# The first quarter of the values loaded on ScalarE's DMA queue, ahead of the bias rows

## The chip, the cores and the metric

The kernel runs on one core of a Trainium2 chip. The metric is device time in microseconds of one execution, as the median of several runs: 118.21 us for the kernel before (three runs, 117.67 to 118.22).

## The reference

Softmax attention in its linear form, for 8 batches, 8 heads, 576 positions and head size 64, followed by a gated ("highway") layer on the 4608 x 512 result:

```python
def _attn_ref(q, k, v):
    q_s = softmax(q, axis=-1)
    k_s = softmax(k, axis=2)            # over the positions
    kv = np.einsum('bhsd,bhse->bhde', k_s, v)
    return np.einsum('bhsd,bhde->bhse', q_s, kv)

def _moe_ref(x, w_h, w_t, b_t):
    H = np.maximum(x @ w_h, 0.0)
    T = 1.0 / (1.0 + np.exp(-(x @ w_t + b_t)))
    return T * H + (1.0 - T) * x
```

`q`, `k`, `v` and the output are float32; the kernel computes in float16 with float32 sums.

## The kernel before, in words

The whole program is one list of steps, `ORDER`. A step is named `kind_batch_part`, with an engine's letter behind a colon where the engine can be chosen (`A` ScalarE, `D` VectorE, `P` GpSimd). The steps are issued in that order, each engine's instructions keep it, and every engine waits for what the instruction at its head needs. The words below use these step names.

Per batch, the steps are: `k`, `v`, `q` load rows from memory (lines 269, 292); `ek` and `eq` take the exponentials on ScalarE (lines 339, 397); `vc` casts the values to float16 (line 345); `kv` multiplies keys by values on TensorE (line 355); `kr` and `kn` normalise that product on VectorE (lines 367, 377); `qt` and `qc` turn the queries, on TensorE and then by a copy (lines 441, 452); `xu`, `rs`, `x` make the attention output (lines 496, 511, 523); `xt` and `xe` turn it (lines 542, 553). The layer behind it is `bw` (gate bias into PSUM, line 564 on TensorE), `mt` and `mh` (the two products, lines 574 and 582), `th`, `dd`, `uu`, `oo`, and `st` (the stores).

In batch 0 the loads come in pieces: two of the queries, `q_0_0` (512 KB) and `q_0_4` (640 KB); two of the keys, `k_0_0` and `k_0_2` (576 KB each); and four of the values, `v_0_0` to `v_0_3` (288 KB each). All go out on SyncE (SP in the profile). The bias row of 2 KB is loaded twice, `b_0` and `b_32` (line 300, into two partitions), on ScalarE's queue. ScalarE and SyncE each have a DMA queue of their own: q10 and q1 in the profile.

What the bias does next: VectorE casts both rows and subtracts (`bsplit`, lines 323 and 324); TensorE spreads the result over the partitions (`bp`, line 330); ScalarE copies it to `ball` (`bc`, line 333). On TensorE `bp` stands behind 13 dummy products (`fill_5`, `fill_8`, line 253) and ahead of `qt_0_0`, two `bw`, eight more dummy products and `kv_0_0`. On VectorE `bsplit` stands ahead of the cast of `v_0_1` and of `qc_0_0`.

Every DMA of SyncE and ScalarE takes one of eight semaphores in turn, so a DMA waits at its issue for the one eight before it to land.

Of the kernel before, what the change touches and what calls it, by code (L numbers as in the profile page):

```python
# [13 lines left out]


ORDER = """
b_0 q_0_0 v_0_1 setupdve k_0_0 b_32 eq_0_0 bsplit setuppool fill_5 fill_8 bp v_0_0 bc qt_0_0 ek_0_1 v_0_3 ek_0_0 k_0_2
v_0_2 vc_0_3:A bw_1 vc_0_0 ek_0_2 vc_0_2 q_0_4 vc_0_1:D ek_0_3 bw_0 w_h_0 fill_8 qc_0_0 whd_1:P kv_0_0 eq_0_1 w_h_2
w_t_2 kr_0_0 whd_0:P whd_2:P wtb_2:P bw_2:D fill_4 w_t_0 q_1_4 k_1_2 kn_0_0 v_1_2 xu_0_0 kv_0_1 kr_0_1 fill_5 kn_0_1
xu_1_0 rs_1_0 k_1_0 wtb_0:P qt_0_1 qc_0_1:A x_1_0 xt_1_0 xe_1_0 xu_0_1 wtb_1:P fill_2 whb_2 v_1_0 whb_1:D rs_0_0 whb_0  # L20
# [45 lines left out]
def kernel(  # L66
# [10 lines left out]
    nc = tc.nc  # L77
# [35 lines left out]
    def once(name, make):  # L113
        if name not in T:
            T[name] = make()
        return T[name]
# [143 lines left out]
    def landing(which, b):  # L260
        return once(f"{which}32{b}", lambda: ld.tile([P, 4, NJ * D], FP32, tag=which, name=f"{which}32_{b}"))

    def rows_of(which, b):
        return source[which][b].rearrange("(c hh) (p j) d -> (hh p) c (j d)", hh=2, p=NP)

    def load_kv(which):
        def step(e, b, c):
            n = (2 if which == "k" else 1, 2)[b] if b < 2 else 4
            nc.sync.dma_start(landing(which, b)[:, c:c + n], rows_of(which, b)[:, c:c + n])
        return step  # L270

    WIDE = (4, 5, 6, 7)
# [363 lines left out]
    def st(e, i, h):  # L636
# [21 lines left out]
        setuppool=setup_pool, setuplate=setup_late, setupdve=setup_dve, bsplit=bsplit, fill=fill,  # L658
# [38 lines left out]
```

## Time and profile before

| What | us |
|---|---|
| median of the runs before | 118.21 |
| runs before, lowest and highest | 117.67, 118.22 |
| the profiled execution, its own time | 118.84 |
| its span in the trace | 117.0 |

The profile page gives each engine's busy time, the share that the DMA engines were busy, and the chain of work that ended last. A row of the timeline is: start in us, duration in us, engine, line, operation, out<-in, and in brackets how long the engine sat idle before it and what ended the wait. "SPq" and "ACTq" rows are DMA issues. In the windows view a row names a stretch and its length, then the busy time of each engine, the granted TensorE clock, the mean busy share of the 16 DMA engines and what they moved in GB/s. The DMA view of a window lists the queues with packets, megabytes and share.

### The profile page before, as it was taken

How to read it: one execution, taken by the hardware profiler on the slowest of the kernel's cores; microseconds unless marked ns; L12 is line 12 of the kernel's file. 1: busy time of each engine (PE TensorE's matmuls, PEld its weight loads, DVE VectorE, ACT ScalarE, POOL GpSimd, SP SyncE). 2: the span in 40 equal slices, each digit the busy share in tenths (PEclk: the TensorE clock that was granted, in tenths of full speed). 3: DMA queues.
4: the chain of work that ended last, by engine and by line, in shares of the span. 5: the costliest groups of instructions: out<-in, count | busy, mean ns of one | idle time of the engine just before them, and what ended most of it. 6: DMA issues, size and time to landing. Idle time of an engine off the chain costs nothing.

```text
span 117.0 us, 3825 instructions
## 1 busy us (share of the span) xinstructions
PE 105.7 (90%) x1544; PEld 56.7 (48%) x1544; DVE 94.7 (81%) x225; ACT 90.2 (77%) x129; POOL 87.1 (74%) x101
## 2 busy tenths in 40 slices
PE   5997866998899999999999999999999989999930
PEld 1353532554556646645474547455454534454520
DVE  5544585597999899999889887997999979899870
ACT  4276393977789899998999986989999958867320
POOL 5011154068999999999899999999899918996760
PEclk9999999999999999999999999999999999999995
DMA  2999999999999999999999999999999999999654
GB/s 48 372 399 378 407 393 382 391 372 387 391 391 391 389 394 362 379 391 365 375 390 380 350 365 404 358 361 335 391 354 259 107 362 325 403 398 352 247 209 177
DMA packets 24197, 40.62 MB, mean 347 GB/s; under 512 B 5362, under 2 KB 11762, under 8 KB 24180
## 3 DMA queue, kind: packets, MB, share of 16 engines
q1 hardware_dynamic: 24032, 40.24, 98.4%
q8 instruction: 12, 0.20, 0.7%
q10 hardware_dynamic: 148, 0.14, 0.3%
q14 instruction: 5, 0.04, 0.1%
HBM read 30.41 MB, written 9.44 MB: 341 GB/s over the span
## 4 chain that ended last, share of the span: by engine, by line
PE 41%; DMA 27%; ACT 19%; DVE 6%; issue 3%; SPq 1%; DVEq 0%; ACTq 0%
DMA q<-in_q_dram 21%; PE one L582 15%; PE one L574 14%; DMA eq<-qe 6%; ACT qe L392 4%; PE one L542 3%; PE one L441 3%; ACT ek L339 3%; ACT one L598 3%; ACT eq L452 2%; PE pair L487 2%; PE pair L355 2%; ACT th L596 2%; ACT eq L454 1%; ACT xT L553 1%
## 5 line engine op out<-in xcount | busy, mean ns | idle before, releaser
L634 POOL TENSOR_TENSOR o<-u,x 128x512 f32<-128x512 f16 (+1 forms) x36 | 40.6, 1143 | 5.9 <-DVE u L616 4.5
L582 PE MATMUL one<-w16h,xT 128*128 128x512 f16 x144 | 36.4, 380 | 0.8 <-ACT xT L553 0.7
L574 PE MATMUL one<-w16t,xT 128*128 128x512 f16 (+1 forms) x148 | 36.9, 374 | 0.2 <-issue 0.2
L602 DVE SCALAR_TENSOR_TENSOR d<-x,one 128x512 f16<-128x512 f16 x36 | 24.1, 673 | 2.0 <-PE one L582 2.0
L614 POOL TENSOR_TENSOR u<-g,d 128x512 f16<-128x512 f16 x18 | 20.8, 1158 | 1.5
L345 POOL CAST v<-v 128x1152 f16<-128x1152 f32 (+1 forms) x11 | 10.6, 972 | 13.5 <-DMA v<-in_v_dram 13.1
L339 ACT ACTIVATE ek<-k 128x576 f16<-128x576 f32 (+2 forms) x15 | 17.9, 1224 | 2.4 <-DMA k<-in_k_dram 2.4
L582 PEld LDWEIGHTS <-xT 128*128 128x128 f16 x144 | 12.7, 98 | 13.7 <-ACT xT L553 1.2
L518 DVE TENSOR_TENSOR x<-pair,rs 128x512 f16<-128x512 f32 x27 | 18.2, 684 | 1.1
L574 PEld LDWEIGHTS <-xT 128*128 128x128 f16 x148 | 13.0, 98 | 11.9 <-issue 0.5
L397 ACT ACTIVATE qe<-q 128x1024 f16<-128x1024 f32 (+3 forms) x9 | 9.4, 1055 | 5.7 <-DMA q<-in_q_dram 5.7
L598 ACT ACTIVATE one<-one 128x512 f32<-128x512 f32 (+1 forms) x19 | 10.7, 562 | 3.1 <-PE one L574 2.7
L616 DVE SCALAR_TENSOR_TENSOR u<-one,d 128x512 f16<-128x512 f32 (+1 forms) x18 | 12.0, 671 | 1.2 <-ACT one L598 0.9
L253 PE MATMUL one<-blank 128*128 128x512 f16 x32 | 9.7, 454 | 2.2 <-POOL blank L143 1.3
L560 ACT COPY one<-ball 128x512 f32<-128x512 f32 x18 | 10.6, 588 | 1.4 <-DVE d L602 0.8
L596 ACT ACTIVATE th<-one 128x512 f16<-128x512 f32 x18 | 10.5, 594 | 1.1 <-PE one L574 0.9
L613 POOL TENSOR_SCALAR g<-th 128x512 f16<-128x512 f16 x18 | 11.2, 622 | 0.1
L542 PE MATMUL one<-idh,x 128*128 128x128 f16 x92 | 9.5, 220 | 1.0 <-DVE x L523 1.0
L562 DVE COPY one<-ball 128x512 f32<-128x512 f32 x13 | 8.9, 684 | 0.6 <-ACT th L596 0.5
L542 PEld LDWEIGHTS <-x 128*128 128x128 f16 x92 | 6.4, 98 | 5.9 <-DVE x L523 2.8
L392 ACT ACTIVATE qe<-q 128x1024 f16<-128x1024 f32 (+1 forms) x7 | 8.2, 1182 | 0.8 <-DMA q<-in_q_dram 0.8
L553 ACT COPY xT<-one 128x512 f16<-128x512 f16 (+1 forms) x10 | 5.5, 546 | 3.3 <-PE one L542 2.7
(68 smaller groups left out, 133.1 us busy)
## 6 DMA issues: line engine op xcount, KB each, us to landing
v<-in_v_dram SPq DMA_DIRECT2D x6, 1152.0 KB, 13.5
k<-in_k_dram SPq DMA_DIRECT2D x6, 1152.0 KB, 11.9
out_dram<-o SPq DMA_DIRECT2D x23, 256.0 KB, 3.7
q<-in_q_dram SPq DMA_DIRECT2D x10, 512.0 KB, 12.4
out_dram<-o SPq DMA_DIRECT2D x6, 512.0 KB, 4.5
k<-in_k_dram SPq DMA_DIRECT2D x4, 576.0 KB, 9.2
q<-in_q_dram SPq DMA_DIRECT2D x2, 1152.0 KB, 15.1
q<-in_q_dram SPq DMA_DIRECT2D x2, 640.0 KB, 9.7
```

The source lines that it names most:

```text
L339: nc.scalar.activation(t[:, :, c:c + n].rearrange("p j c d -> p c j d"), T[f"k32{b}"][:, c:c + n].rearrange("p c (j d) -> p c j d", j=NJ), ...
L392: nc.scalar.activation(t[:, half].rearrange("p t c d -> p c t d"), src, AF.Exp)
L518: nc.vector.tensor_mul(t.rearrange("p k (w h) e -> p w k h e", w=2), pairs(i)[:, :, :, 1:129].rearrange("p w k (h e) -> p w k h e", h=2), ...
L542: nc.tensor.matmul(t[:, n], T[f"x{i}"][:, n0 + n % 2:n0 + 2 * P:2], idh, is_transpose=True, start=True, stop=True, skip_group_check=True)
L574: nc.tensor.matmul(T[gate(i, k)][:, cs], T[f"xT{i}"][:, n], w16["t"][:, n, cs], start=False, stop=(n == parts[-1] and not first), skip_gro ...
L582: nc.tensor.matmul(t, T[f"xT{i}"][:, n], w16["h"][:, n], start=(first and n == parts[0]), stop=(n == parts[-1] and not (first and len(part ...
L596: nc.scalar.activation(T[f"th{i}"], src, AF.Tanh, scale=0.5)
L598: nc.scalar.activation(src, src, AF.Tanh, scale=0.5)
L602: nc.vector.scalar_tensor_tensor(t, T[f"x{i}"], -0.5, T[f"gps{i}"], op0=ALU.mult, op1=ALU.max)
L614: nc.gpsimd.tensor_mul(t, g, T[f"d{i}"])
L616: nc.vector.scalar_tensor_tensor(t[:, cs], T[gate(i, h)][:, cs], 1.0, T[f"d{i}"][:, cs], op0=ALU.add, op1=ALU.mult)
L634: eng.tensor_add(t[:, cs], T[f"u{i}_{h}"][:, cs], T[f"x{i}"][:, cs])
```

## The change

`v_0_1` gets the letter `A` and moves to the front of the list, and the loader takes ScalarE's queue for a step with that letter. SyncE issues one load fewer at the start, and ScalarE issues `v_0_1` ahead of the two bias rows.

```diff
 ORDER = """
-b_0 q_0_0 v_0_1 setupdve k_0_0 b_32 eq_0_0 bsplit setuppool fill_5 fill_8 bp v_0_0 bc qt_0_0 ek_0_1 v_0_3 ek_0_0 k_0_2
+v_0_1:A b_0 q_0_0 setupdve k_0_0 b_32 eq_0_0 bsplit setuppool fill_5 fill_8 bp v_0_0 bc qt_0_0 ek_0_1 v_0_3 ek_0_0 k_0_2
...
     def load_kv(which):
         def step(e, b, c):
             n = (2 if which == "k" else 1, 2)[b] if b < 2 else 4
-            nc.sync.dma_start(landing(which, b)[:, c:c + n], rows_of(which, b)[:, c:c + n])
+            (nc.scalar if e == "A" else nc.sync).dma_start(landing(which, b)[:, c:c + n], rows_of(which, b)[:, c:c + n])
         return step
```

The first rows of ScalarE's program before (a name's first number is the batch; the last is only a buffer's number):

```order
L300 DMA b_86<-in_moe_b_t_dram 1x512 x2
L397 ACT_TABLE_LOAD
L397 ACTIVATE qe_120<-q_0_101 128x4x4x64
L333 COPY ball<-one_160 128x512
L339 ACTIVATE ek_174<-k_0_117 128x9x64 x2
```

and with the change:

```order
L269 DMA v_0_100<-in_v_dram 128x576
L300 DMA b_86<-in_moe_b_t_dram 1x512 x2
L397 ACT_TABLE_LOAD
L397 ACTIVATE qe_120<-q_0_103 128x4x4x64
L333 COPY ball<-one_160 128x512
L339 ACTIVATE ek_174<-k_0_117 128x9x64 x2
```

The load of the values, 128 rows of 576 numbers, now stands ahead of the two bias loads, and nothing else moves on ScalarE.

The first rows of SyncE's program before:

```order
L292 DMA q_0_101<-in_q_dram 128x4x256
L269 DMA v_0_103<-in_v_dram 128x576
L269 DMA k_0_117<-in_k_dram 128x2x576
L269 DMA v_0_103<-in_v_dram 128x576 x2
L269 DMA k_0_117<-in_k_dram 128x2x576
L269 DMA v_0_103<-in_v_dram 128x576
L292 DMA q_0_101<-in_q_dram 128x4x320
```

and with the change:

```order
L292 DMA q_0_103<-in_q_dram 128x4x256
L269 DMA k_0_117<-in_k_dram 128x2x576
L269 DMA v_0_100<-in_v_dram 128x576 x2
L269 DMA k_0_117<-in_k_dram 128x2x576
L269 DMA v_0_100<-in_v_dram 128x576
L292 DMA q_0_103<-in_q_dram 128x4x320
```

The second row is gone; each later load is one place nearer to the front of SyncE's queue. TensorE's instructions are the same, and on VectorE and GpSimd only the number of the values' buffer differs. In the turn of eight semaphores the load of `v_0_2` (the last `v` row of SyncE above) waited for `b_0`, and now waits for `v_0_1`.

## The prediction

> **What bounds the kernel now.** I read the page first, then busy time by stage, then the chain.
>
> ```profile
> PE 105.7 (90%) x1544; PEld 56.7 (48%) x1544; DVE 94.7 (81%) x225; ACT 90.2 (77%) x129; POOL 87.1 (74%) x101
> DMA  2999999999999999999999999999999999999654
> q1 hardware_dynamic: 24032, 40.24, 98.4%
> PE 41%; DMA 27%; ACT 19%; DVE 6%; issue 3%; SPq 1%; DVEq 0%; ACTq 0%
> ```
>
> The reader should see that two resources are nearly full over the whole span: TensorE (90%) and the DMA engines (98.4% by queue q1, 9 tenths in every slice but the first and the last three). The windows (PE busy is the first column after the length, the DMA share the last but one) show where TensorE is not full:
>
> ```profile
> 0.00:14.00 14.00, 11.55 (x120) 5.36 (x120) 6.61 (x25) 7.14 (x9) 2.94 (x11) 1.00 0.88 317
> 14.00:20.00 6.00, 3.79 (x32) 2.00 (x33) 4.65 (x13) 4.01 (x8) 3.24 (x6) 1.00 1.04 390
> 20.00:30.00 10.00, 9.48 (x134) 5.44 (x132) 7.46 (x19) 7.67 (x13) 5.03 (x6) 1.00 1.06 383
> 90.00:100.00 10.00, 9.52 (x158) 4.65 (x157) 9.11 (x19) 7.58 (x12) 7.17 (x8) 1.00 0.99 261
> ```
>
> From 20 us on TensorE has at most half a microsecond idle in ten. So an event in the first 15 us, where the change lies, moves the end by about what it moves the start of that dense stretch. The chain there:
>
> ```profile
> 0.73 4.39 DMA q<-in_q_dram
> 5.14 7.81 DMA q<-in_q_dram
> 12.97 1.07 ACT qe L397
> 19.75 1.04 PE one L582 x4
> ```
>
> The reader should see that the chain runs through the landing of the second piece of the queries, not through the values that are moved: the cast of `v_0_1` (VectorE, 5.91, below) is not in it.
>
> **The change, part by part.** These rows are the start of the two queues and the bias work:
>
> ```profile
> 0.73 0.78 ACTq L300 DMA_DIRECT2D b<-in_moe_b_t_dram  x2
> 0.73 0.46 SPq L292 DMA_DIRECT2D q<-in_q_dram  x1
> 1.25 0.49 SPq L269 DMA_DIRECT2D v<-in_v_dram  x1
> 1.54 1.28 ACT L397 ACT_TABLE_LOAD   x1 [1.54 <-PEq L681]
> 4.67 0.42 DVE L323 CAST b<-b 1x512 f16<-1x512 f32 x1 [1.32 <-DMA b<-in_moe_b_t_dram]
> 5.13 0.68 DVE L324 TENSOR_TENSOR b<-b,b 1x512 f16<-1x512 f32 x1
> 4.06 0.47 SPq L269 DMA_DIRECT2D v<-in_v_dram  x1
> 5.15 1.06 ACT L397 ACTIVATE qe<-q 128x1024 f16<-128x1024 f32 x1 [2.32 <-DMA q<-in_q_dram]
> 5.91 0.75 DVE L345 CAST v<-v 128x576 f16<-128x576 f32 x1
> ```
>
> *Issue.* SyncE loses one issue of 0.49 us. That is worth nothing: SyncE's queue is issued far ahead of its data (`q_0_4`, issued at 5.14, lands 7.81 us later), so the data in front of it hide the earlier issue. For the same reason the new wait of `v_0_2` for `v_0_1` costs nothing. `v_0_1` has landed by 5.91 already now, so the issue of `v_0_2` and of what is queued behind it on SyncE (`q_0_4`, then the weights) slips at most from 4.06 to about 5.9, while GpSimd gets the data of `v_0_2` only at 11.21 (the row stands below with the other casts). ScalarE gains that 0.49 us ahead of its bias issues and its table load, which then ends near 3.3; its first work waits for the queries until 5.15 anyway. `v_0_1` landing earlier helps nobody: `kv_0_0`, the first user, starts at 9.23.
>
> *The order of the data.* This is what costs. In the DMA view for 1.9 to 4.0 us, and then for 4.0 to 4.2 us, the queues read:
>
> ```profile
> DMA packets 452, 0.47 MB, mean 222 GB/s; under 512 B 4, under 2 KB 446, under 8 KB 452
> q1 hardware_dynamic: 452, 0.47, 86.2%
> ```
>
> ```profile
> q1 hardware_dynamic: 60, 0.08, 104.3%
> q10 hardware_dynamic: 2, 0.00, 2.8%
> ```
>
> `b_32` was issued by 1.51, yet from 1.9 to 4.0 us no packet of q10 ran at all; its two packets (the row and its signal) ran after 4.0, as the first piece of the queries was ending. So a transfer of one queue waited until its DMA engine was through with the other queue's whole transfer. The last stores say the same. Here are their issues, and the queues from 114.7 to 115.2 us:
>
> ```profile
> 113.55 0.51 SPq L642 DMA_DIRECT2D out_dram<-o  x1
> 113.61 0.38 ACTq L642 DMA_DIRECT2D out_dram<-o  x1
> ```
>
> ```profile
> q10 hardware_dynamic: 119, 0.12, 68.3%
> q1 hardware_dynamic: 43, 0.04, 24.6%
> ```
>
> ScalarE's store, issued 0.06 us later, ran ahead of SyncE's in a block. I read both as: an engine takes a whole transfer of the one queue, then one of the other. With the change the turns are then `v_0_1` and `q_0_0`, `b_0`, `k_0_0`, `b_32`: the second bias row comes behind 288 KB of values and 576 KB of keys more than now. What 288 KB take is the distance of the first two landings here:
>
> ```profile
> 8.19 0.66 POOL L345 CAST v<-v 128x576 f16<-128x576 f32 x1 [5.91 <-DMA v<-in_v_dram]
> 8.91 0.67 ACT L345 CAST v<-v 128x576 f16<-128x576 f32 x1 [0.25 <-DMA v<-in_v_dram]
> 11.21 0.67 POOL L345 CAST v<-v 128x576 f16<-128x576 f32 x1 [2.35 <-DMA v<-in_v_dram]
> ```
>
> 0.72 us; three times that is 2.16. Against it stands the slow start. From 1.9 to 4.0 the engines moved 222 GB/s where 394 is the mean of 4.2 to 20 us,
>
> ```profile
> DMA packets 2967, 6.23 MB, mean 394 GB/s; under 512 B 199, under 2 KB 1251, under 8 KB 2966
> ```
>
> so 2.1 x (1 - 222/394) = 0.92 us of transfer were lost, some of which a second queue with work may fill. I take 0.3 of it, nearer to nothing than to all, since nothing shows that the gaps are the queue's and not the engines'. **The bias lands 2.16 - 0.3 = 1.86 us later**; the ends are 2.16 - 0.92 = 1.24 and, where the queries go ahead of the values on that engine and one more 288 KB comes in between, 2.88.
>
> The Trainium skill, "DMA: Bandwidth & Descriptors", section "Issuing engines are not separate DMA queues", says that issuing from several engines saves only the sequencer's issue time. By that the 0.3 would be 0 and the bias 2.16 us late; no row here shows two full queues at the start.
>
> *What a late bias delays.* On TensorE:
>
> ```profile
> 6.11 0.59 PE L330 MATMUL one<-b,ones 128*128 128x512 f16 x2
> 9.23 0.48 PE L355 MATMUL pair<-v,ek 64*64 64x65 f16 x36
> 11.09 0.28 PE L496 MATMUL one<-kvb,eq 128*128 128x130 f16 x2 [0.40 <-DVE kvb L377]
> 11.93 0.48 PE L355 MATMUL pair<-v,ek 64*64 64x65 f16 x36 [0.56 <-POOL v L345]
> 14.09 0.62 PE L441 MATMUL one<-idh,qe 128*128 128x128 f16 x8 [0.26 <-ACT qe L397]
> ```
>
> The bias is ready at 5.13 + 0.68 = 5.81, and `bp` starts at 6.11 when the dummy products end: 0.30 of cover. Behind `bp` stand `qt_0_0`, two `bw` and eight dummy products in fixed order, so `kv_0_0` moves with it, and so do VectorE's `kr` and `kn` and the `xu` of 11.09. The next product, `kv_0_1`, had waited 0.56 for its values, and `qt_0_1` 0.26 for its exponentials; both idle times are eaten first. What is left reaches the chain at 14.09: 1.86 - 0.30 - 0.56 - 0.26 = **0.74 us**; with the two ends 0.12 and 1.76. ScalarE's `bc` and `ek` slide within this. `q_0_0`, which may land up to 0.72 later behind the values, is hidden too: `qt_0_0` then stands behind the late `bp`. From there to 19.75, where the chain's row begins the dense stretch, TensorE waits often (3.79 us busy of 6), but by the view of waits on VectorE, ScalarE and its own issue and never on a load. So I take nothing off and count 0.7 to the end.
>
> **The sum.** The profiled execution took 118.84 (span 117.0 and 1.84 around it), which is 0.63 above the median. 118.84 + 0.7 = 119.5 for an execution like it, and 118.21 + 0.7 = **118.9** for the median.
>
> **The rivals.**
>
> *The queues alternate in small portions, and the start is filled* (faster). The Trainium skill's same page, section "Queues, rings and completion order", says that an engine switches queues at packets, typically 9 to 17 descriptors. As a mechanism of this kernel: ScalarE's queue holds only the 8 rows per engine of `v_0_1` ahead of the bias, so the bias would land no later than 4.67, nothing would be eaten, and the stream of loads could start up to 0.92 earlier, which moves `q_0_4` at 12.95 and the chain behind it. Half of that gives 118.21 - 0.4 = 117.8, the ends 117.3 and 118.2. For it: the share and rate at the start, 222 against 394 GB/s. Against it: the 2.1 us without a packet of q10.
>
> *The late bias is absorbed* (no change). Later idle times that a DMA ends,
>
> ```profile
> 79.10 1.06 ACT L392 ACTIVATE qe<-q 128x1024 f16<-128x1024 f32 x1 [0.55 <-DMA q<-in_q_dram]
> 94.75 0.30 PE L487 MATMUL pair<-kvl,eq 64*128 64x65 f16 x8 [0.48 <-DMA eq<-qe]
> ```
>
> could swallow 0.5 us of 0.7, if the stream of loads is not late itself: 118.4, between 118.0 and 118.8. Against it: ScalarE issues the second of those transposes only after its own work, which would be late too.
>
> **How the numbers follow.** A change of 0.5%, 0.6 us, is about what a measurement of this kernel can tell from none. The forecast has a chance of 0.55; its ends, 118.3 to 120.0, put 0.37 above 118.8 and 0.18 within 0.5%. The first rival has 0.27: 0.18 faster by over 0.5%, 0.09 within. The second has 0.18: 0.13 within, 0.05 slower. Together: faster 0.18, same 0.40, slower 0.42. The range reaches from most of the first rival's cases to the greater part of the forecast's: 117.6 to 119.7.
>
> **What would show it.** In the new profile VectorE's cast of the second bias row should start near 6.5 (from 6.0 to 7.5) instead of 4.67, `bp` near 7.7, `kv_0_0` near 10.8, the `qt` of 14.09 near 14.8, the product of 19.75 near 20.4. If the cast starts before 5 us, the turns of whole transfers are wrong. If it is late and the product of 19.75 is not, the idle times were larger than I read. If both are late and the end is not, the dense stretch has more room than its busy shares say.

## The result, and the profile after

The change makes the kernel slightly slower. The median of 22 runs is 118.42 us (118.15 to 118.66) against 118.20 us (117.67 to 119.50, 22 runs) for the kernel before. The ratio is 1.0023, with a 95% interval of 1.0012 to 1.0034: 0.27 us more, with 0.14 to 0.40 as the interval. The profiled execution took 118.21 us, with a span of 116.4. That is 0.63 less than the execution that was profiled before, so the two must not be subtracted: four executions of each kernel are laid side by side below.

From the page of the kernel with the change, the busy times, the DMA row in 40 slices, the queues, and the shares of the chain:

```profile
PE 106.0 (91%) x1544; PEld 56.6 (49%) x1544; DVE 94.4 (81%) x225; ACT 90.1 (77%) x129; POOL 86.9 (75%) x101
...
DMA  3999999999999999999999999999999999997654
...
q1 hardware_dynamic: 23888, 39.95, 97.2%
q10 hardware_dynamic: 292, 0.43, 1.1%
q8 instruction: 12, 0.20, 0.7%
...
PE 80%; DVE 8%; DMA 4%; ACT 3%; issue 1%; ACTq 1%; DVEq 0%
```

The same two resources are full. New is the chain: the share of DMA fell from 27% to 4% and TensorE's doubled. The chain of waits with the change, by start and duration, tells why:

```profile
1.76 4.47 DMA b<-in_moe_b_t_dram
...
6.25 0.43 DVE b L323
...
6.71 0.69 DVE b L324
...
7.44 0.59 PE one L330 x2
...
8.91 1.73 PE one L253 x8
10.64 0.45 PE pair L355 x33
...
20.22 1.04 PE one L582 x4
```

The path no longer starts with the queries. It starts with the bias row of 2 KB, whose landing takes 4.47 us, goes through VectorE's cast and subtraction into `bp`, and from there along TensorE through the eight dummy products to `kv_0_0`. So the moved values are still not on the path, but the bias behind them now is.

The timeline with the change at the places named in the prediction:

```profile
0.74 0.43 ACTq L269 DMA_DIRECT2D v<-in_v_dram  x1
0.74 0.47 SPq L292 DMA_DIRECT2D q<-in_q_dram  x1
1.20 0.82 ACTq L300 DMA_DIRECT2D b<-in_moe_b_t_dram  x2
...
2.05 1.28 ACT L397 ACT_TABLE_LOAD   x1 [2.05 <-issue]
...
5.05 1.06 ACT L397 ACTIVATE qe<-q 128x1024 f16<-128x1024 f32 x1 [1.72 <-DMA q<-in_q_dram]
6.25 0.42 DVE L323 CAST b<-b 1x512 f16<-1x512 f32 x1 [1.29 <-DMA b<-in_moe_b_t_dram]
...
7.44 0.59 PE L330 MATMUL one<-b,ones 128*128 128x512 f16 x2 [0.66 <-DVE b L324]
10.57 0.48 PE L355 MATMUL pair<-v,ek 64*64 64x65 f16 x36
12.42 0.28 PE L496 MATMUL one<-kvb,eq 128*128 128x130 f16 x2 [0.40 <-DVE kvb L377]
12.63 0.48 PE L355 MATMUL pair<-v,ek 64*64 64x65 f16 x36
...
14.13 0.40 PE L496 MATMUL pair<-kvb,eq 128*128 128x130 f16 x4
14.36 0.61 PE L441 MATMUL one<-idh,qe 128*128 128x128 f16 x8
```

The cast of the second bias row starts at 6.25 instead of 4.67, `bp` at 7.44 instead of 6.11, and `kv_0_0` at 10.57 instead of 9.23. `kv_0_1` has lost its wait for values and starts 0.70 later, and the `qt` of 14.09 has lost its wait for exponentials and starts 0.27 later. The queries, which the prediction let slip by up to 0.72, are not late here: their exponentials start at 5.05, against 5.15.

Where the second bias row stood can be read in the DMA view of the changed kernel for 1.9 to 4.0 us (packets, MB, share),

```profile
DMA packets 490, 0.64 MB, mean 304 GB/s; under 512 B 16, under 2 KB 370, under 8 KB 490
...
q1 hardware_dynamic: 354, 0.36, 52.6%
q10 hardware_dynamic: 136, 0.28, 41.7%
```

for 3.9 to 4.2 us,

```profile
q1 hardware_dynamic: 111, 0.11, 106.4%
q10 hardware_dynamic: 2, 0.00, 1.9%
```

for 4.2 to 5.2 us,

```profile
q1 hardware_dynamic: 235, 0.39, 109.2%
```

for 5.2 to 5.4 us,

```profile
q1 hardware_dynamic: 30, 0.07, 92.1%
q10 hardware_dynamic: 1, 0.00, 16.6%
```

and for the whole of 4.7 to 5.65 us:

```profile
DMA packets 147, 0.34 MB, mean 356 GB/s; under 512 B 0, under 2 KB 0, under 8 KB 147
```

First the values (q10) and the queries (q1) share the start, at 304 GB/s where one queue alone moved 222. Two packets of q10 follow near 4 us, the first row and its signal. From 4.2 to 5.2 us there is no packet of q10 at all, though both bias rows had been issued by 2.02: q1 moves the keys. The next packet of q10, the second row, comes after 5.2 us. So the order in which the transfers begin is the one that the prediction read: values and queries, first row, keys, second row.

But the second row does not stand behind the whole of the keys. In the trace a transfer like that of the keys ends with 16 packets of 4 bytes, one for each DMA engine, its signals. From 4.7 to 5.65 us no packet under 512 B was moved, so no engine had finished its share of the keys when the row's packet started, at 5.29. In the three other traces of the change (in the table below) it started at 5.43, 5.96 and 5.74, and the first signal of the keys followed at 5.75, 5.98 and 6.01.

The following table is read from the timelines of four executions of each kernel (start in us; the first column of each four is the profiled execution of that kernel; the others are e1, e14 and e15 of before, and e9, e12 and e13 of the change, all told below):

```
                        before                       with the change
1st bias row, cast       3.00  3.00  3.00  3.00       4.55  4.72  5.09  5.01
2nd bias row, cast       4.67  4.75  4.99  4.87       6.25  6.10  6.58  6.41
queries, exponentials    5.15  5.25  5.63  4.67       5.05  5.16  5.49  5.74
bp                       6.11  5.93  6.18  6.08       7.44  7.29  7.77  7.59
kv_0_0                   9.23  9.07  9.45  9.21      10.57 10.42 10.89 10.72
kv_0_1                  11.93 12.03 12.41 12.00      12.63 12.47 12.95 12.78
2nd piece of queries    12.97 13.08 13.45 13.04      13.04 12.23 12.56 12.81
qt of 14.09             14.09 14.20 14.56 14.15      14.36 14.21 14.69 14.52
mh of 19.75             19.75 19.87 20.23 19.82      20.22 19.98 20.45 20.35
last mt                111.91 111.31 111.90 111.85   111.35 111.34 111.82 111.59
time of the execution  118.84 118.19 118.78 118.73   118.21 118.21 118.75 118.46
```

By the means, the lateness is 1.52 us at the cast of the second row, 1.45 at `bp`, 1.41 at `kv_0_0`, 0.62 at `kv_0_1`, 0.20 at the `qt`, 0.33 at the start of the dense stretch, and none at the last `mt`. (In all of them the time is the start of the last `mt` plus 6.86 to 6.93.) The exponentials of the queries' second piece start 0.47 earlier by the means, though not in the profiled execution. The 0.27 us of the 22 runs cannot be seen in four executions, which differ by 0.65 among themselves.

### The profile page after: what moved, and what is told of

Read it like the earlier page. It is cut to its first block, busy times and chain, and to the rows that moved or that the text cites. A ratio compares the mean times of both kernels' runs of the same rounds, so it can differ in the third digit from the quotient of the medians.

```text
span 116.4 us, 3825 instructions
## 1 busy us (share of the span) xinstructions
PE 106.0 (91%) x1544; PEld 56.6 (49%) x1544; DVE 94.4 (81%) x225; ACT 90.1 (77%) x129; POOL 86.9 (75%) x101
## 4 chain that ended last, share of the span: by engine, by line
PE 80%; DVE 8%; DMA 4%; ACT 3%; issue 1%; ACTq 1%; DVEq 0%
PE one L574 27%; PE one L582 26%; PE pair L355 5%; PE one L542 5%; PE pair L487 4%; DMA b<-in_moe_b_t_dram 4%; PE one L441 4%; PE one L253 3%; PE pair L534 2%; PE pair L496 1%; DVE x L523 1%; PE pair L415 1%; DVE d L602 1%; ACT w16h L319 1%; DVE kvb L377 1%
## 5 line engine op out<-in xcount | busy, mean ns | idle before, releaser
L253 PE MATMUL one<-blank 128*128 128x512 f16 x32 | 10.2, 473 | 1.9 <-POOL blank L143 1.3
```

The costliest lines, as they stand in the source:

```text
L253: nc.tensor.matmul(space("early", 1), blank[:, 0:P], blank, start=True, stop=True, skip_group_check=True)
```

## The experiments

Theory A: the late bias is what costs, since it holds `bp` and all of TensorE's work behind it. Theory B: the place of the values in the stream of loads costs something by itself. Theory C, formed from the first traces: a small lateness is swallowed late in the program by a wait of TensorE that sets the time in steps.

**e1_before_again** is the kernel before, unchanged, for the scatter between executions.

> The kernel before, unchanged, for a second trace of it: the first one was of an execution of 118.84 us, 0.6 above the median. Both theories expect 118.2 and a span near 116.4. If the dense stretch on TensorE still starts at 19.75 us and ends some 0.3 us earlier than with the change, the 0.47 us by which the change starts it later are lost on the way by 0.2; if the 53 to 66 us idle times of TensorE are gone here, they belonged to that one execution.

Measured: 118.19 us. It is the second column of the table.

**e2_bias_first** and **e10_bias_first_again** keep the values on ScalarE's queue but issue both bias rows ahead of them:

```diff
-v_0_1:A b_0 q_0_0 setupdve k_0_0 b_32 eq_0_0 bsplit
+b_0 b_32 v_0_1:A q_0_0 setupdve k_0_0 eq_0_0 bsplit
```

> The change, but with both bias loads issued ahead of the values on ScalarE's queue. Theory A (the late bias delays TensorE's first products, and that is all): the bias cast starts by 4.7 us again, the first key-value product at 9.2, and the time is that before, 118.2, ratio 0.998 to 1.001. Theory B (two queues at the start disturb the stream of loads, and the late bias is covered): the values still come on the second queue, one DMA engine still lags, and the time stays at 118.45, ratio 1.002.

> The change with both bias loads ahead of the values, as before, on the chip of the change itself. Theory A: ratio 0.999 to 1.000. Theory B: ratio 1.002, that of the change.

Measured: 118.17 us, ratio 0.9992 (0.9972 to 1.0013), and in the repeat 118.54 us, ratio 1.0013 (0.9987 to 1.0038). The timeline of the first, at the cast, `bp`, `kv_0_0` and the product of 19.75:

```profile
4.50 0.42 DVE L323 CAST b<-b 1x512 f16<-1x512 f32 x1 [1.15 <-DMA b<-in_moe_b_t_dram]
...
6.83 0.64 PE L330 MATMUL one<-b,ones 128*128 128x512 f16 x2
...
10.01 0.48 PE L355 MATMUL pair<-v,ek 64*64 64x65 f16 x36
...
19.56 1.04 PE L582 MATMUL one<-w16h,xT 128*128 128x512 f16 x4 [0.68 <-ACT xT L553]
```

The bias is on time again, as A has it, so its lateness does come from its place behind the values and the keys. In the trace of the repeat, an execution of 119.31 us, it is less so: the cast starts at 5.33, 0.34 behind the latest of the four before. The times settle nothing: both intervals hold 1, and that of the repeat holds the ratio of the change as well. Beside the repeat, in the same session, the change itself (e9 below) gave 1.0010; theory A had expected it 0.2 to 0.3 us above the repeat's 1.0013, and that difference did not show. Two more things are seen in the first of the two. `bp` starts at 6.83 although the bias was ready by 6, because the dummy products ahead of it ran longer at the low clock (see the last section); and `kv_0_0` is 0.94 later than in e1_before_again, yet the dense stretch starts 0.31 earlier. In this execution nearly a microsecond at `kv_0_0` is free, though the exponentials of the queries' second piece also come 0.32 earlier (12.76 against 13.08).

The repeat shows how a DMA engine shares two queues that both have rows waiting. From 5.4 to 5.9 us the values (q10) are moved beside the loads of SyncE (q1):

```profile
q1 hardware_dynamic: 49, 0.11, 57.0%
q10 hardware_dynamic: 38, 0.09, 43.1%
```

In the trace each packet starts as another ends, so the packets can be strung into 16 chains, one for each engine. In these chains each of the 128 rows of the values is followed by a packet of q1, and never by another row of the values. So an engine alternates between the queues packet by packet; it does not finish a transfer of one queue first.

**e3_six_more, e11_ten_more, e5_seventeen_more** are the kernel before, with 6, 10 and 17 dummy products more ahead of `kv_0_0`. They make TensorE late without touching a load:

```diff
-w_h_0 fill_8 qc_0_0 whd_1:P kv_0_0
+w_h_0 fill_14 qc_0_0 whd_1:P kv_0_0
```

(and `fill_18`, `fill_25`).

> The kernel before, with six dummy products more (8 to 14) between the gate biases and the first key-value product; loads untouched. Six at 0.215 us delay that product by 1.29 us, as the change does (10.57 against 9.23). Theory A: the time of the change, 118.4 to 118.5, ratio 1.002, with the product of 19.75 us at 20.2. Theory B: 118.2, ratio 1.000.

> The kernel before, with ten dummy products more (8 to 18) ahead of the first key-value product: 2.15 us, between the runs with six and with seventeen. Theory A1 (early lateness first eats about 1 us of idle time before 15 us, then a fixed 0.3 to 0.6 later): the dense stretch starts 1.2 later, the end moves by 0.6 to 0.9, ratio 1.005 to 1.008. Theory A2 (later waits swallow about half of it): dense stretch the same, end 0.6. Theory B (the loads set the end): under 0.3.

> The kernel before, with 17 dummy products more (8 to 25) ahead of the first key-value product, which delays it by 17 x 0.215 = 3.65 us; loads untouched. The dense stretch, at 19.75 us before, should start some 2.7 us later, after about 1 us of idle time is eaten. Theory A1 (waits for loads later on swallow a fixed 0.2 to 0.3 us): the end moves by 2.4, to 120.6. Theory A2 (they swallow about half): 1.3, to 119.5. Theory B (the stream of loads sets the end, and early lateness of TensorE does not matter): under 0.4, to 118.6 at most.

Measured: 118.47 us, ratio 1.0017 (0.9994 to 1.0041); 119.79, ratio 1.0108 (1.0065 to 1.0151); 120.48, ratio 1.0186 (1.0145 to 1.0228). How late `kv_0_0` and the product of 19.75 are is read from rows like these, in the timeline of TensorE with ten dummy products more,

```profile
12.17 0.48 PE L355 MATMUL pair<-v,ek 64*64 64x65 f16 x36
...
21.97 1.04 PE L582 MATMUL one<-w16h,xT 128*128 128x512 f16 x4 [0.68 <-ACT xT L553]
```

and with seventeen more:

```profile
13.56 0.48 PE L355 MATMUL pair<-v,ek 64*64 64x65 f16 x36
...
23.38 1.04 PE L582 MATMUL one<-w16h,xT 128*128 128x512 f16 x4 [0.68 <-ACT xT L553]
```

**e6_bias_late** is the kernel before with both bias rows on SyncE's queue, behind the keys and the first values:

```diff
-b_0 q_0_0 v_0_1 setupdve k_0_0 b_32 eq_0_0
+q_0_0 v_0_1 setupdve k_0_0 v_0_0 b_0 b_32 eq_0_0
...
-        nc.scalar.dma_start(b32[r:r + 1], moe_b_t.rearrange("(o n) -> o n", o=1))
+        nc.sync.dma_start(b32[r:r + 1], moe_b_t.rearrange("(o n) -> o n", o=1))
```

> The kernel before, with both bias loads on SyncE's queue behind the load of v_0_0, so that nothing but the bias is moved; its cast should start near 8.3 us instead of 4.7 and the first key-value product near 12.8, as in the run with 17 dummy products more. If a late bias acts only through TensorE's order, the time is that of that run within 0.3 us. If not, what differs is due to the loads or to the other engines that wait for the bias.

Measured: 122.16 us, ratio 1.0321 (1.0274 to 1.0368). Its `bp` in the timeline, and then three windows (PE busy first, the granted clock third from the end):

```profile
10.21 1.01 PE L330 MATMUL one<-b,ones 128*128 128x512 f16 x2 [3.22 <-DVE b L324]
```

```profile
8.00:10.00 2.00, 0.00 (x0) 0.00 (x0) 1.75 (x3) 0.00 (x0) 0.66 (x1) 1.00 1.05 389
10.00:12.00 2.00, 1.78 (x11) 1.23 (x11) 0.92 (x2) 1.16 (x3) 0.67 (x1) 0.56 1.07 374
12.00:14.00 2.00, 2.00 (x7) 0.70 (x6) 0.69 (x1) 2.00 (x5) 0.00 (x0) 0.59 1.04 410
```

The cast of the second row starts at 9.03, 4.28 later than in e1_before_again, and the kernel is 3.8 us slower. That is 1.7 us more than with seventeen dummy products, where 0.3 at most had been expected. TensorE waits 3.22 us for the bias, and then pays a second time: the granted clock falls to about half for 3.4 us, just after the wait, which makes `kv_0_0` 5.94 late.

The five kernels that make `kv_0_0` late, against e1_before_again (for the change, the means of the table):

```
                     kv_0_0 late   dense stretch late   by the ratio
e3_six_more             1.29            0.15            0.2 (-0.1 to 0.5)
the change              1.41            0.33            0.27 (0.14 to 0.40)
e11_ten_more            3.10            2.10            1.3 (0.8 to 1.8)
e5_seventeen_more       4.49            3.51            2.2 (1.7 to 2.7)
e6_bias_late            5.94            4.70            3.8 (3.3 to 4.4)
```

About 1.0 to 1.2 us of lateness is eaten before 20 us in each; beyond that it comes through to the dense stretch, and 0.8 to 1.3 us of the three larger ones are eaten later. The last column goes by medians, though, and the other two by single executions. By the times of the profiled executions themselves (120.00, 121.11 and 122.24, against 118.19) only 0.3 to 0.7 us is eaten later. So a late bias does cost, and the change lies just at the foot of this curve: its 1.41 us is 0.2 to 0.4 more than the idle time ahead can eat.

**e4_fills_ahead** is the change, with six of the dummy products moved from behind `bp` to ahead of it, so that the wait for the bias is filled and what follows `bp` is shorter:

```diff
-eq_0_0 bsplit setuppool fill_5 fill_8 bp v_0_0
+eq_0_0 bsplit setuppool fill_5 fill_14 bp v_0_0
...
-w_h_0 fill_8 qc_0_0 whd_1:P kv_0_0
+w_h_0 fill_2 qc_0_0 whd_1:P kv_0_0
```

> The change, with six of the eight dummy products that stand between the bias product and the first key-value product moved ahead of the bias product, where TensorE waits for the bias. The number of products is the same. Theory A: the first key-value product is back at 9.2 to 9.4 us and the time at 118.2, ratio 1.000. Theory B: 118.45, ratio 1.002.

Measured: 118.03 us, ratio 1.0004 (0.9981 to 1.0027). The bias is as late as in the change (cast at 6.45, `bp` at 7.70), `kv_0_0` starts at 9.91, after a wait of 0.30 us for the exponentials of the keys, and the dense stretch at 19.57. The lateness at the dense stretch is gone, and so is a measurable difference from the kernel before. This agrees with A, but the interval does not exclude the change's own ratio.

**e7_keys_split** is the change with the first 576 KB of keys loaded in two pieces and the second bias row issued between them:

```diff
-v_0_1:A b_0 q_0_0 setupdve k_0_0 b_32 eq_0_0
+v_0_1:A b_0 q_0_0 setupdve k_0_0 b_32 k_0_1 eq_0_0
...
-            n = (2 if which == "k" else 1, 2)[b] if b < 2 else 4
+            n = (2 if which == "k" and c == 2 else 1, 2)[b] if b < 2 else 4
```

> The change, with the first load of the keys (576 KB) cut into two of 288 KB. If an engine takes whole transfers of the two queues in turn, the second bias row now waits for half as much of the keys: its cast starts near 5.5 us instead of 6.25, the first key-value product near 9.8 instead of 10.6, and the time is 118.2 to 118.3. If the turn is not by transfers, the cast stays at 6.25 and the time at 118.4.

Measured: 118.37 us, ratio 0.9994 (0.9972 to 1.0017). In its timeline

```profile
5.74 1.06 ACT L397 ACTIVATE qe<-q 128x1024 f16<-128x1024 f32 x1 [2.42 <-DMA q<-in_q_dram]
5.90 0.42 DVE L323 CAST b<-b 1x512 f16<-1x512 f32 x1 [0.81 <-DMA b<-in_moe_b_t_dram]
```

the second bias row comes 0.16 us behind the queries, against 6.25 - 5.05 = 1.20 with the change. Most of that difference is the queries, which are 0.69 later in this execution. Against the first row, whose cast starts at 4.68, the second comes 1.22 us later; in the four traces of the change it is 1.70, 1.38, 1.49 and 1.40. ScalarE's queue is the same in all; only the size of the other queue's transfer has halved. So that size counts, but the row came 0.16 to 0.48 us closer and not the 0.72 that 288 KB of data take, and its cast started at 5.90, where 5.5 had been expected. One execution can't say more, and it does not show that an engine takes whole transfers in turn.

**e8_six_fewer** is the kernel before with six dummy products fewer (`fill_2` in place of the second `fill_8`), to see whether an earlier `kv_0_0` gains.

> The kernel before, with six dummy products fewer (8 to 2) ahead of the first key-value product, which then starts 1.3 us earlier. The next one still waits for its values until 11.9, so every theory here expects no gain: 118.2, ratio 0.998 to 1.002. If it is faster, TensorE's early order bounds the kernel before as well; if it is slower, the dummy products kept TensorE's clock up.

Measured: 118.53 us, ratio 0.9998 (0.9969 to 1.0027). It tells little on an earlier start. `kv_0_0` started at 8.82, only 0.25 earlier, after a wait of 1.05 us for its values, and something else came in between. The windows of its profiled execution:

```profile
10.00:12.00 2.00, 0.69 (x17) 0.34 (x18) 0.60 (x3) 1.26 (x2) 0.67 (x1) 0.91 1.08 376
12.00:14.00 2.00, 2.00 (x40) 1.00 (x36) 0.75 (x3) 1.06 (x1) 0.00 (x0) 0.50 1.02 406
```

With fewer dummy products TensorE was busy 0.69 of 2 us, the clock halved, and the dense stretch started at 20.82, 0.95 later than in e1_before_again.

**e9_change_again** is the change once more.

> The change itself, beside the kernel with the bias first on the same chip, since the difference in question is as small as one execution's spread. Theory A (only the late bias costs): 118.4 to 118.5, ratio 1.002, and above the kernel with the bias first by 0.2 to 0.3 us. Theory B (the second queue itself costs): the two are equal.

Measured: 118.44 us, ratio 1.0010 (0.9986 to 1.0034). The interval overlaps that of the first measurement; alone it would not show a difference.

**e12_change_look, e13_change_look** (the change) and **e14_before_look, e15_before_look** (the kernel before) are single executions, to see where the lateness at 20 us goes.

> A further trace of the change. In nine traces of several kernels TensorE stood still before its matmul number 862 (a boundary of 256 instructions, two for each matmul) and went on at 65.2, 65.4, 65.7 or 65.9 us, though the products ahead of it ended at quite different distances. Theory C (that wait for its next block of instructions decides which of the times 117.95, 118.2, 118.45 an execution takes): an execution of 118.4 to 118.5 shows 862 at 65.9, one of 118.2 at 65.7. Theory D (later events decide): 862 at 65.7 in either.

> The same as the run before, once more: theory C, the time and the start of matmul 862 go together in steps of 0.25 us; theory D, they do not.

> A further trace of the kernel before. Theory C: an execution of 117.95 shows matmul 862 at 65.4, one of 118.2 at 65.7, one of 118.45 at 65.9. Theory D: no such order.

> The same as the run before, once more, with the same expectations of both theories.

Measured: 118.75, 118.46, 118.78 and 118.73 us. The place is TensorE's product number 862. These are the timelines of TensorE there, of e1_before_again (the kernel before),

```profile
65.10 0.40 PE L542 MATMUL one<-idh,x 128*128 128x128 f16 x4
65.66 1.02 PE L574 MATMUL one<-w16t,xT 128*128 128x512 f16 x4 [0.16 <-issue]
```

of the profiled execution of the change,

```profile
65.25 0.40 PE L542 MATMUL one<-idh,x 128*128 128x128 f16 x4
65.68 1.02 PE L574 MATMUL one<-w16t,xT 128*128 128x512 f16 x4
```

and of e9_change_again (the change):

```profile
65.00 0.40 PE L542 MATMUL one<-idh,x 128*128 128x128 f16 x4
65.67 1.02 PE L574 MATMUL one<-w16t,xT 128*128 128x512 f16 x4 [0.27 <-issue]
```

TensorE reaches this product at 65.40, 65.50 or 65.65 and starts it at 65.66 to 65.68 each time, after a wait that nothing in the profile ends. From there the three run alike and end at 118.19 to 118.21. Up to 0.25 us of lateness is swallowed here. e5, e6 and e8, which come more than 1.5 us later, don't wait at all; e11, 1.6 us later, waits 0.29 again. The start does not take just any value. Over thirteen executions, of both kernels and of the experiments that stay close to them, it was near 65.2, 65.4, 65.66, 65.9 or 66.18, and where later waits were alike the time followed (e13_change_look: 65.92 and 118.46). In e12 and e14 the profile shows a second such wait, at product 1118, of 0.30 and 0.44 us, and in the profiled execution of before two waits at line 487 of 0.24 and 0.48; these three took 118.75 to 118.84. So C holds for executions whose later waits are alike. It does not explain the result of the runs: why the change ends about one such step later on the average stays open.

## Why the prediction was right or wrong

The prediction had the direction, and it had the main path: a late bias, late by its place in the two queues, which makes TensorE's first products late. It had the size wrong: 0.7 us, where 0.27 us was measured (118.9 and 118.42 as medians). The step that failed is the idle time that a late bias meets on TensorE: 0.56 + 0.26 = 0.82 us was counted, and 0.79 + 0.42 = 1.21 was there. The way in which an engine shares two queues was misread as well. Its steps:

- *Issue, costed at nothing.* Right. ScalarE's table load ended at 3.3 and its first work waited 1.72 us for the queries; SyncE's later loads were not held up, up to the queries' second piece (issued at 5.05, before at 5.14).
- *The turns of whole transfers.* Right as an order, wrong as a mechanism. The second row did come late, with the keys in between. But engines alternate between the queues packet by packet (e10), and the row's packet started at 5.29 while every engine still had rows of the keys to move. What kept a row that had been issued by 2.02 from its engine until then, no run isolates. So the near hit on the lateness, 1.86 for 1.52, is in part luck. The first rival, small portions, had the sharing right and the consequence wrong: it put the bias no later than 4.67, and the cast started at 6.10 to 6.58.
- *"The bias lands 2.16 - 0.3 = 1.86 us later".* It was 1.52. By the table the first row with the change stands where the second stood before (4.84 and 4.82 as means), so the values ahead cost nothing, where 0.72 - 0.3 = 0.42 was forecast; from the first row to the second it was 1.49, near the 1.44 for the keys. The fuller start does not explain all of this. From 1.9 to 4.0 us two queues moved 304, 286, 239 and 233 GB/s in the four traces and one queue 222, 230, 169 and 248. By the means that is 0.10 MB more, or 0.26 us at 394 GB/s, close to the 0.3; what hid the rest stays open. The Trainium skill, "DMA: Bandwidth & Descriptors", section "Issuing engines are not separate DMA queues", by which this term would be zero, is not borne out at the start of this program; afterwards, with a deep queue, 392 GB/s with the change and 394 without is no difference.
- *The cover of 0.30.* It was 0.07 at `bp` as a mean, and 0.04 more went on the way to `kv_0_0`. It is set by the end of the dummy products, which varies from execution to execution with the clock: by the same working it is 0.30 in the profiled execution of before and 0.04 to 0.07 in the other three. With the change, where TensorE waits for the bias, `bp` starts 0.04 behind it as well, so 0.04 is no cover.
- *"Both idle times are eaten first"; 0.74 reaches the chain at 14.09.* This is the step that failed. 1.41 came to `kv_0_0`, where 1.56 was forecast. On the way to `kv_0_1` 0.79 of it was eaten instead of 0.56, and on the way to the `qt` another 0.42 instead of 0.26, so that 0.20 reached the chain and 0.33 the dense stretch. Two things were misread. A row's idle time is counted from the end of the row ahead, but where nothing waits the next product starts before that end: with the change `kv_0_1` starts at 12.63, where the row ahead ends at 12.42 + 0.28 = 12.70, and the `qt` at 14.36, where it ends at 14.13 + 0.40 = 14.53. So even in the execution that was read the room was 0.64 and 0.43 us, not 0.56 and 0.26. And at the first place that execution had little of it: in it `kv_0_1` follows `kv_0_0` after 2.70 us, in the other three after 2.79 to 2.96; with the change it is 2.05 or 2.06 each time, with no idle time left. At the second place the four of before agree, 2.15 to 2.17 us from `kv_0_1` to the `qt`, and 1.73 or 1.74 with the change.
- *"So I take nothing off and count 0.7 to the end."* For the change itself, 0.33 at the dense stretch and 0.27 (0.14 to 0.40) in the runs agree with it, though in the four traces nothing of it is left at the last `mt`. For the larger doses it is wrong: by the medians 2.10 became 1.3 and 3.51 became 2.2, by the profiled executions 1.8 and 2.9. The prediction had listed late waits that could swallow lateness, for the second rival, but only those that a DMA ends; the wait at product 862 stands under "issue" and so had no name in the view of waits.
- *The base.* The profiled execution, 118.84 us, was slower than 20 of the 22 runs of before. The sum was set against the median instead, which was right; but its idle times were taken as the kernel's, which was not.
- *The rivals.* The second, "the late bias is absorbed", named the size of the result (118.4) for a reason that the runs do not bear out: most was absorbed ahead of 20 us, by waits for values and exponentials, and not by late waits for a DMA.

Not settled: whether all of the measured 0.27 us is the bias. The late `kv_0_0` of e3, without any change to the loads, gives 0.2 with an interval that holds both zero and 0.27, and the two runs with the bias first disagree. Nor is it settled what the fuller start is worth. In three of the four traces of the change the exponentials of the queries' second piece started at 12.23 to 12.81, against 12.97 to 13.45 before. In the profiled execution they did not, for one of the 16 DMA engines: 15 had signalled this piece by 12.27 (12.87 before), the last at 13.02 (12.95 before). Why that one lagged was not tried. e2 and e4, with the values on the second queue and the bias on time or covered, reached the dense stretch at 19.56 and 19.57, ahead of all four traces of before, but e10 only at 19.94, and none of the three is measurably faster.

## What to carry to other kernels

A tiny load on a second queue is not independent of the first: here its packet ran 3.3 us after its issue, when two big transfers of the other queue had begun ahead of it, so its place is to be counted in transfers, and it belongs in front of a big one of its own queue. When an event at the head of a program moves, read the idle time ahead of the dense part in several executions, not in one, and from start to start rather than from the gaps that the rows print; and take a gap that stands under "issue" in the dense part as room too. Differences of 0.2% then need a dose that is several times larger (here the added dummy products) to be seen as cause and effect.

## What the runs showed of the hardware that was not expected

**Two queues fill the start better, and their packets alternate one by one.** As means of four traces each, 266 GB/s from 1.9 to 4.0 us with a second queue and 217 without; but single traces range from 233 to 304 and from 169 to 248. In e10 each of 128 rows of one queue was followed by a packet of the other. Even so a 2 KB row, issued by 2.02 us, ran only at 5.29.

**TensorE waits at fixed numbers of products.** The wait stays at product 862 also where added dummy products move another line there (in e3 and e11 a product of line 487, not 574), and the next is at 1118, 256 products or, with their weight loads, 512 instructions on. A queue named "instruction" moved 12 packets with 0.20 MB, some 16 KB each, in the whole span, one of them in the 3 us before that wait. In the DMA view of e1_before_again for 62.5 to 64.6 us:

```profile
q1 hardware_dynamic: 913, 0.75, 106.8%
q8 instruction: 1, 0.02, 3.0%
```

I take it that TensorE waits for the next block of its program, whose packet has to pass the loads on a DMA engine. This is argued, not shown: no run changed the instructions' path alone, and this packet was through by 64.4, 1.3 us before TensorE went on at 65.66. The Trainium skill, "Runtime: NRT & Kernel Launch", section "Instruction fetch mechanics", says that each engine's program is refilled in blocks of 16 KB over a DMA queue of its own, and calls the cost mostly hidden; the packets of 16 KB agree, the waits of 0.2 to 0.6 us with full DMA queues would be where it is not. It puts 256 instructions into a block, so that 862 and 1118 would be two blocks apart; e10 has a wait of 0.15 us at the product half way, 990, too.

**The clock starts and falls at its own time.** In the traced executions TensorE's granted clock rose to full between 4.3 and 6.9 us, though the dummy products began at 1.3 in each, and with it the start of `bp` moved from 5.87 to 6.84 in kernels whose bias was on time. In e6 it fell after 3.22 us of idle time, and in e8 after a stretch that was only mostly idle, in both cases for 3.4 us: TensorE had been busy for 0.2 and 1.7 of the 3.4 us ahead of the fall. By the clock records of all 17 traces each later change comes a whole number of 3.41 us after the rise, one in e6 (6.82 to 10.23), two in e8 (4.81 to 11.63). The Trainium skill, "TensorE: Matmul & The Clock Gate", section "What's actually happening", describes a free-running window of 3.4 us; the scatter of the rise, these distances and the length of both falls agree with it.
